# Attention with a SwiGLU feed-forward: keys as three chunks of 128 and a shared rest of 64, products in two banks

## The chip, the cores and the metric

The kernel runs on one core of a Trainium2 chip. The metric is the device time of one execution in microseconds (us), the median of several runs. The engines are TensorE (PE in the profile; PEld are its weight loads), VectorE (DVE), ScalarE (ACT), GpSimd (POOL) and SyncE (SP, which issues DMAs here).

## The reference

Multi-head attention over 8 batches of 12 heads, 448 positions of 64, then a feed-forward with a gate on the 3584 rows of 768. All tensors are float32; the kernel computes in float16 with float32 sums.

```python
q, k, v: (8, 12, 448, 64)
scores = np.matmul(q, k.transpose(0, 1, 3, 2)) / np.sqrt(64)
attn = softmax(scores)                                # over the keys
x = np.matmul(attn, v).transpose(0, 2, 1, 3).reshape(3584, 768)
g = x @ w_gate                                        # (768, 1536)
out = (g * sigmoid(g) * (x @ w_val)) @ w_out          # (1536, 768)
```

## The kernel before

Two heads make a pair: 48 pairs, six to a batch. Pair `pr` goes through these steps. Queries and keys are loaded as float16, position `4 p + c` at partition `p` of 112, chunk `c` of 4. They are turned so that the head dimension lies on partitions, head 0 on 0 to 63 and head 1 on 64 to 127 (on TensorE for the first pairs, by a DMA transpose from pair 11 on). `qk` makes the scores of one chunk of keys for both heads and takes their exponential:

```python
ps_s = ctx.enter_context(tc.tile_pool(name="ps_s", bufs=3, space=PSUM))   # tag "s": 3 tiles of two banks
ps_f = ctx.enter_context(tc.tile_pool(name="ps_f", bufs=2, space=PSUM))   # tag "f": 2 tiles of one bank

def qk(pr, c):                                  # c = 0..3, P = 112, S = 448, D = 64
    t = qkT[pr]
    s = ps_s.tile([128, 2, 512], FP32, tag="s")
    for hx in range(2):
        nc.tensor.matmul(                       # L217
            s[:, hx, 0:S],
            lhsT=t[ts(hx, 64), c * P : c * P + 128],
            rhs=t[ts(hx, 64), ds(S + (1 - hx) * D, S)],
            start=True,
            stop=True,
        )
    e = Es[pr % NE][:, ds(c * EB, 16)].rearrange("p (h b) x -> p h (b x)", h=2)
    nc.scalar.activation(e[:, :, 0:S], s[0:P, :, 0:S], AF.Exp, scale=sm_scale)      # L225
```

`pv_chunk` multiplies the exponentials with V. V has a column of ones behind its 64, so the sums of the softmax come with it as column 65. Both heads' 7 blocks of results (128 queries each; the last block holds the last 64 queries of both) lie in one bank, a tile of pool "f":

```python
def pv_chunk(pr, c):
    if c == 0:
        accs[pr] = ps_f.tile([128, 512], FP32, tag="f", name="acc")
    ...
    for j in range(3):
        for hx in range(2):
            nc.tensor.matmul(                   # L243
                a7[:, 2 * j + hx],
                lhsT=e[:, ds(c * EB + 9 * hx + 2 * j, 2)].rearrange("p b x -> p (b x)"),
                rhs=vo[:, hx, c, 0 : D + 1],
                start=c + j + hx == 0,
                stop=False,
            )
    for hx in range(2):
        nc.tensor.matmul(a7[:, 6], ...)         # L251
    if c < NC - 1:
        return
    ...
    nc.vector.reciprocal(r[:, 0:7], a7[:, :, D])          # L262
    nc.vector.tensor_tensor(xt[:, 0:n], a7[:, 0:n, 0:D], ..., ALU.mult)   # L264
```

The results are turned (`turn_x`, a DMA transpose from pair 12 on) into X, the input of the feed-forward. Its work is a list of steps. An FFN1 step takes one of 12 blocks of 128 hidden columns: six matmuls for the gate into `gp` (pool "s"), six for the value into `vp` (pool "f"), one activation on ScalarE and two operations on VectorE, of which the second, `hts`, reads `vp` out. An FFN2 step is twelve matmuls into `op` (pool "f"), which ScalarE copies to `osb`. The feed-forward of a batch's rows comes in blocks of 384 and of 512 rows.

The queues of all engines follow one list of visits. A visit has two or three chunks of scores, then the product of a pair whose exponentials are all there (none where no pair is ready), then some feed-forward steps of an earlier batch:

```python
for x, (chunks, todo) in enumerate(plan):
    for pr, c in chunks:
        qk(pr, c)
    ...
    for _, p0 in todo:
        pv(p0)
        ...
    if adds[max(y for y in adds if y <= x)] < 2:
        ...
        carry = run_budget(left() / (end - x) + carry)
    else:
        at, n = count["at"], count["visits"]
        no = share(count["o"], at, n)
        nf = 1
        ...
        for y in range(nf):
            if fvq:
                run_fv()
        for _ in range(no):
            run_o()
```

The last block of rows has nothing beside it and runs alone at the end.

Of the kernel before, what the change touches and what calls it, by code (L numbers as in the profile page):

```python
# [17 lines left out]
NB = 2  # L18
# [8 lines left out]
NX = 6  # L27
NV = 5
VS = 9
EB = 15  # L30


@with_exitstack
def kernel(
# [24 lines left out]
    MQ = S - D  # L59

# [22 lines left out]

    Es = [consts.tile([P, NC * EB + 1, D], FP16, name=f"E{i}") for i in range(NE)]
    Xts = [consts.tile([128, 7, D], FP16, name=f"xt{i}") for i in range(NX)]
    Xrs = [consts.tile([D, 128], FP16, name=f"xr{i}") for i in range(3)]
    Vts = [consts.tile([P, 2, NC, D + 2], FP16, name=f"vo{i}") for i in range(NV)]
    vraw = consts.tile([P, VS, 2, NC, D], FP16, name="vraw")
# [30 lines left out]

    def load_qk16(pr, n=2):  # L120
        h0 = 2 * (pr % 2) if pr >= 14 else 0
        if h0 == 0:
            q16 = raws.tile([P, 4, NC, D], FP16, tag="rq", bufs=RB, name="q16")
            k16 = raws.tile([P, 4, NC, D], FP16, tag="rk", bufs=RB, name="k16")
            pairbuf[:] = [q16, k16]
        q16, k16 = pairbuf
        for dst, src in ((q16, q), (k16, k)):
            flat = src.rearrange("b h s d -> (b h) s d")[2 * pr : 2 * pr + 2 * n]
            nc.gpsimd.dma_start(dst[:, ds(h0, 2 * n)], flat.rearrange("h (p c) d -> p h (c d)", c=NC))  # L129
        for i in range(n):  # L130
            h = h0 + 2 * i
            raw[pr + i] = (q16[:, h : h + 2], k16[:, h : h + 2])

    def load_v(pr, n=1):
        b, h = divmod(2 * pr, H)
        nc.gpsimd.dma_start(  # L136
            vraw[:, ds(pr % VS, n)].rearrange("p r h c d -> p (r h) (c d)"),
            v[b, h : h + 2 * n].rearrange("h (p c) d -> p h (c d)", c=NC),
        )

    def copy_v(pr):
        nc.vector.tensor_copy(Vts[pr % NV][:, :, :, 0:D], vraw[:, pr % VS])  # L142

# [12 lines left out]

    def prep(pr):
        rq, rk = raw[pr]
        if pr == 0 or pr >= NPE:
            qk16 = attp.tile([P, 2, NC, 2, D], FP16, tag="qk16", bufs=3)  # L160
# [7 lines left out]
        qkT[pr] = attp.tile([128, 2 * S + D], FP16, tag="qkT", name="qkT", bufs=5)  # L168
        if pr >= NPE:
            nc.sync.dma_start_transpose(  # L170
                qkT[pr][:, 0 : 2 * S].rearrange("p (c q) -> p c q", q=P),
                qk16[:].rearrange("p t c h d -> p (t c h d)"),
# [39 lines left out]

    def qk(pr, c):
        t = qkT[pr]
# [20 lines left out]
    def pv_chunk(pr, c):  # L235
# [3 lines left out]
        vo = Vts[pr % NV]  # L239
# [20 lines left out]
        r = attp.tile([128, 8], FP32, tag="R", bufs=2, name="R")  # L260
        xt = Xts[pr % NX]
        nc.vector.reciprocal(r[:, 0:7], a7[:, :, D])  # L262
        n = 7 if pr < XPE else 6
# [6 lines left out]
        if pr < XPE:  # L270
            return
        for hx in range(2):
            nc.vector.tensor_scalar(
                Xrs[pr % 3][:, ts(hx, D)], a7[ts(hx, D), 6, 0:D], r[ts(hx, D), 6:7], None, ALU.mult
            )

    def pv(pr):
        for c in range(NC):
            pv_chunk(pr, c)

    def turn_x(pr):
# [6 lines left out]
        if pr < XPE:  # L288
# [12 lines left out]
            dst[:, 0:MQ].rearrange("p (j q) -> p j q", j=3),  # L301
            xt[:, 0:6].rearrange("p j d -> p (j d)"),
        )
        nc.sync.dma_start_transpose(dst[:, MQ:S].rearrange("p (j q) -> p j q", j=1), Xrs[pr % 3][:])
# [48 lines left out]
    def ffn2_steps(kk, c0, n, hts, first, last_block):  # L353
# [6 lines left out]
        for ch, oh in steps:  # L360
# [7 lines left out]
            for m0, w in parts:  # L368
# [16 lines left out]
                while l < l0 + 128:  # L385
                    b, j = divmod(l, S)
                    c, p0 = divmod((j + D) % S, P)
                    m = min(P - p0, l0 + 128 - l, (MQ if j < MQ else S) - j)
# [16 lines left out]
    with tc.manual_schedule():  # L405
        load_qk32(0)
        nc.vector.memset(warm[:], 0.0)
        for e in Es:
# [41 lines left out]
        def add_block(i, visits):  # L450
# [5 lines left out]
            (oq if i == 0 else ffn2_wait).extend(own)  # L456
            count.update(visits=visits, fv=NFB, o=len(oq), at=0, more=NFB - visits)
# [53 lines left out]
        queue = []  # L511
        for p0 in range(FIRST, NPAIR):
            queue.append((NC * p0 + NC, p0))
        plan = []
        g = FIRST * NC
        last = NPAIR * NC
        while g < last or queue:
            n = 2 if g < WIDE * NC else 3
            todo = []
            while queue and queue[0][0] <= g and len(todo) < 2:  # L520
# [121 lines left out]
```

The softmax here doesn't subtract the row's maximum and nothing guards it: scores larger than these inputs give would overflow.

## Time and profile before

| | |
|---|---|
| median of 3 runs | 453.67 us (453.22 to 453.94) |
| span of the profiled execution | 451.7 us, 9871 instructions |
| score matmuls (L217) | 384, 50.6 us busy |
| product matmuls (L243, L251) | 1152 and 384, 53.0 and 42.9 us busy |
| FFN1 matmuls (L326), FFN2 matmuls (L371) | 1152 and 684, 249.3 and 116.1 us busy |
| exponentials (L225) | 192 of 919 ns |
| K, Q and V loads by GpSimd from DRAM | 44, 44 and 42 issues of some 0.66 us |

How to read it: busy time of an engine is the time in which at least one of its instructions is under way, and matmuls overlap, so a busy time divided by a count is not the time of one. A group's row gives line, engine, operation, output and input with their shapes, the count, busy us and the mean ns of one, and then how long the engine stood idle just before and what ended that. A row of waits gives who waited for what: us in total, times, longest. A row of a timeline gives start and length in us and how many instructions were merged into it. A row of windows gives the stretch, its length, then for PE, PEld, DVE, ACT and POOL the busy us and the count, and then the granted clock, the share of DMA and GB/s.

### The profile page before, as it was taken

To read this page: it belongs to the slowest core of one execution; us is meant where nothing else is said; L and a number is where in the kernel's file an instruction comes from. 1 tells how busy PE (TensorE), PEld (TensorE's weight loads), DVE (VectorE), ACT (ScalarE), POOL (GpSimd) and SP (SyncE) were. 2 spreads that over 40 slices of the span, in tenths; PEclk is the share of its full clock that TensorE was granted. 3 is DMA by queue.
4 is the path that set the end of the run, shared out by engine and by line. 5 is a ranking of instruction groups with operands and counts; after the bars stand their busy time and mean duration, and the time that the engine had idled before them with its cause. 6 is when DMAs were issued, how large, how long until landed. Compare 5 with 4: busy or idle time off the path is not lost.

```text
span 451.7 us, 9871 instructions
## 1 busy us (share of the span) xinstructions
PE 441.9 (98%) x4024; PEld 247.0 (55%) x4024; DVE 201.6 (45%) x447; ACT 238.8 (53%) x350; POOL 141.8 (31%) x228
## 2 busy tenths in 40 slices
PE   8999999999999999999999999999999999999995
PEld 3655565545455556454555656545455666544563
DVE  3666562456654434455443534353453544055300
ACT  6965666566746465554554546644555462222221
POOL 8755715927642225252313405330100000000000
PEclk9999999999999999999999999999999999999999
DMA  9999999999969379874749758772503112200033
GB/s 142 173 200 201 196 172 174 180 209 119 145 93 133 46 129 124 132 120 71 126 74 120 98 78 143 118 105 68 101 20 68 46 46 57 70 2 0 17 100 95
DMA packets 105101, 48.71 MB, mean 108 GB/s; under 512 B 59744, under 2 KB 101600, under 8 KB 105056
## 3 DMA queue, kind: packets, MB, share of 16 engines
q0 software_dynamic: 43392, 23.37, 41.2%
q1 hardware_dynamic: 61664, 24.71, 28.9%
q8 instruction: 31, 0.51, 0.5%
q14 instruction: 14, 0.11, 0.1%
HBM read 47.19 MB, written 11.01 MB: 129 GB/s over the span
## 4 chain that ended last, share of the span: by engine, by line
PE 93%; DVE 3%; ACT 2%; issue 1%; DVEq 0%; ACTq 0%
PE op L371 24%; PE gp L326 23%; PE vp L326 23%; PE s L217 9%; PE acc L243 9%; PE acc L251 2%; ACT E L225 2%; PE tp L208 1%; PE wp L109 1%; DVE t L345 1%; ACT sg L341 1%; DVE qkT L209 0%; DVE xt L264 0%; PE acc L291 0%; DVE hts L348 0%
## 5 line engine op out<-in xcount | busy, mean ns | idle before, releaser
L225 ACT ACTIVATE E<-s 112x896 f16<-112x896 f32 x192 | 162.1, 919 | 27.5 <-PE s L217 27.4
L326 PE MATMUL gp<-X,wg 128*128 128x384 f16 (+1 forms) x576 | 124.7, 352 | 0.0
L326 PE MATMUL vp<-X,wv 128*128 128x384 f16 (+1 forms) x576 | 124.6, 352 | 0.0
L371 PE MATMUL op<-wo,hts 128*128 128x384 f16 (+1 forms) x684 | 116.1, 323 | 0.0
L345 DVE SCALAR_TENSOR_TENSOR t<-sg,gp 128x384 f32<-128x384 f32 (+1 forms) x96 | 59.7, 621 | 121.8 <-ACT sg L341 121.8
L341 ACT ACTIVATE sg<-gp 128x384 f32<-128x384 f32 (+1 forms) x96 | 52.5, 547 | 84.8 <-PE gp L326 83.6
L371 PEld LDWEIGHTS <-hts 128*128 128x128 f16 x684 | 65.5, 98 | 45.9 <-issue 3.9
L326 PEld LDWEIGHTS <-wv 128*128 128x128 f16 x576 | 56.3, 98 | 52.6
L326 PEld LDWEIGHTS <-wg 128*128 128x128 f16 x576 | 53.1, 97 | 45.6 <-issue 1.1
L378 ACT ACTIVATE osb<-op 128x384 f32<-128x384 f32 (+1 forms) x57 | 27.8, 487 | 92.5 <-PE op L371 92.5
L167 POOL COPY qk<-q 112x512 f16<-112x512 f16 x37 | 22.9, 619 | 144.5 <-DMA qkT<-qk 143.1
L348 DVE SCALAR_TENSOR_TENSOR hts<-t,vp 128x384 f16<-128x384 f32 (+1 forms) x96 | 59.6, 621 | 10.0
L243 PEld LDWEIGHTS <-E 112*128 112x128 f16 x1152 | 46.7, 97 | 18.2 <-issue 17.5
L243 PE MATMUL acc<-vo,E 112*128 112x65 f16 x1152 | 53.0, 193 | 1.3 <-DVE vo L142 0.7
L217 PE MATMUL s<-qkT 64*128 64x448 f16 x384 | 50.6, 355 | 0.2
L251 PE MATMUL acc<-vo,E 112*128 112x65 f16 x384 | 42.9, 193 | 0.0
L262 DVE RECIPROCAL R<-acc 128x7 f32<-128x7 f32 x48 | 9.8, 205 | 70.6 <-PE acc L251 70.5
L129 POOL DMA_DIRECT2D k<-in_k_dram x44 | 29.0, 660 | 9.5 <-DMA wo<-in_moe_w_out_dram 7.8
L129 POOL DMA_DIRECT2D q<-in_q_dram x44 | 29.3, 666 | 5.2 <-PE s L217 2.5
L136 POOL DMA_DIRECT2D vraw<-in_v_dram x42 | 28.0, 666 | 8.4 <-DVE vo L142 7.2
L217 PEld LDWEIGHTS <-qkT 64*128 64x128 f16 x384 | 14.5, 94 | 25.8 <-issue 18.6
L264 DVE TENSOR_TENSOR xt<-acc,R 128x384 f16<-128x384 f32 (+1 forms) x48 | 27.6, 574 | 1.7
(41 smaller groups left out, 148.2 us busy)
## 6 DMA issues: line engine op xcount, KB each, us to landing
q<-in_q_dram POOLq DMA_DIRECT2D x41, 112.0 KB, 4.0
k<-in_k_dram POOLq DMA_DIRECT2D x41, 112.0 KB, 4.6
vraw<-in_v_dram POOLq DMA_DIRECT2D x39, 112.0 KB, 4.6
wg<-in_moe_w_gate_dram POOLq DMA_DIRECT2D x8, 288.0 KB, 10.1
wv<-in_moe_w_val_dram POOLq DMA_DIRECT2D x8, 288.0 KB, 10.2
wo<-in_moe_w_out_dram POOLq DMA_DIRECT2D x2, 1152.0 KB, 22.0
out_dram<-osb SPq DMA_DIRECT2D x8, 288.0 KB, 3.0
out_dram<-osb SPq DMA_DIRECT2D x8, 240.0 KB, 3.1
```

The costliest lines, as they stand in the source:

```text
L129: nc.gpsimd.dma_start(dst[:, ds(h0, 2 * n)], flat.rearrange("h (p c) d -> p h (c d)", c=NC))
L136: nc.gpsimd.dma_start(vraw[:, ds(pr % VS, n)].rearrange("p r h c d -> p (r h) (c d)"), v[b, h : h + 2 * n].rearrange("h (p c) d -> p h (c ...
L217: nc.tensor.matmul(s[:, hx, 0:S], lhsT=t[ts(hx, 64), c * P : c * P + 128], rhs=t[ts(hx, 64), ds(S + (1 - hx) * D, S)], start=True, stop=True,)
L225: nc.scalar.activation(e[:, :, 0:S], s[0:P, :, 0:S], AF.Exp, scale=sm_scale)
L243: nc.tensor.matmul(a7[:, 2 * j + hx], lhsT=e[:, ds(c * EB + 9 * hx + 2 * j, 2)].rearrange("p b x -> p (b x)"), rhs=vo[:, hx, c, 0 : D + 1] ...
L251: nc.tensor.matmul(a7[:, 6], lhsT=e[:, ds(c * EB + 6 + hx, 2)].rearrange("p b x -> p (b x)"), rhs=vo[:, hx, c, 0 : D + 1], start=False, st ...
L326: nc.tensor.matmul(dst[:, 0:n], lhsT=wslice(kind, fb, cb), rhs=X[kk][:, cb, ds(c0, n)], start=(cb == 0), stop=(cb == NCB - 1),)
L341: nc.scalar.activation(sg[:, 0:n], gp[:, 0:n], AF.Tanh, scale=0.5)
L345: nc.vector.scalar_tensor_tensor(t1[:, 0:n], sg[:, 0:n], 1.0, gp[:, 0:n], ALU.add, ALU.mult)
L348: nc.vector.scalar_tensor_tensor(hts[:, fb, 0:n], t1[:, 0:n], 0.5 * HS, vp[:, 0:n], ALU.mult, ALU.mult)
L371: nc.tensor.matmul(op[:, 0:w], lhsT=hts[:, fb, ts(ch, 128)], rhs=wo[oh][:, fb, ds(m0 - oh * OH, w)], start=(fb == 0), stop=(fb == NFB - 1),)
L378: nc.scalar.activation(osb[:, ds(m0, w)], op[:, 0:w], AF.Copy, scale=1.0 / HS)
```

## The change

From pair 12 on (batches 2 to 7) keys and values are cut otherwise. The 448 keys of a head are 64 groups of seven. They lie on 128 partitions: on the lower 64 the first four of each group, on the upper 64 the last four, so that the fourth is there twice. Of this three chunks of 128 keys and a rest of 64 are taken; of the two heads of a pair one has its rest on the lower half, the other on the upper. The rests of two pairs, four heads, fill one tile of scores and take one exponential. So two pairs have seven tiles of scores and seven exponentials instead of eight. The product of a pair goes into two banks, one per head, which are both tiles of pool "f" (the last two pairs take a tile of pool "s"). The products of the rest, which have 64 rows, come first and directly behind the scores of the visit, the two heads by turns.

With the larger chunks the list of visits is shorter, and from block 2 on the feed-forward steps are spread over the visits by their time; a visit ahead of a product gets an FFN2 step, which comes last in it, where there is one. K and V are loaded in two DMAs of 64 partitions each. The turning of keys and queries is two DMA transposes as before, cut otherwise. Output rows of batches 2 to 7 are in their natural order.

The diff, cut to its core:

```diff
+    def load_keys(eng, dst, src, h0, n):
+        for s in range(2):
+            rows = bass.AP(
+                src.tensor, (h0 * S + s * KR) * D, [[(2 * NC - 1) * D, 64], [S * D, n], [1, NC * D]]
+            )
+            eng.dma_start(dst[ts(s, 64)], rows)
+
+    def low(pr, hx):
+        return hx == pr % 2
...
+    def qk_quad(pr, c):
+        s = ps_s.tile([128, 2, 512], FP32, tag="s")
+        if c < KR:                                                   # KR = 3
+            t = qkT[pr]
+            for hx in range(2):
+                nc.tensor.matmul(
+                    s[:, hx, 0:S],
+                    lhsT=t[ts(hx, 64), ts(c + low(pr, hx), 128)],
+                    rhs=t[ts(hx, 64), ds(NC * 128, S)],
+                    start=True,
+                    stop=True,
+                )
+            e = Eq[pr % NE][:, c]
+        else:
+            for hx in range(2):
+                for p in (pr, pr + 1):
+                    lo = low(p, hx)
+                    t = qkT[p]
+                    nc.tensor.matmul(
+                        s[ts(1 - lo, 64), hx, 0:S],
+                        lhsT=t[ts(hx, 64), ds(0 if lo else KR * 128 + 64, 64)],
+                        rhs=t[ts(hx, 64), ds(NC * 128, S)],
+                        start=True,
+                        stop=True,
+                    )
+            e = Eq[pr % NE][:, RU]
+        nc.scalar.activation(
+            e[:, 0 : 2 * S].rearrange("p (h q) -> p h q", h=2), s[:, :, 0:S], AF.Exp, scale=sm_scale
+        )
...
+    def pv_mm(pr, hx, c, j):
+        lo = low(pr, hx)
+        first = not accs[pr][1][hx]
+        accs[pr][1][hx] += 1
+        if c < KR:
+            rows, e, col = slice(0, 128), Eq[pr % NE][:, c], c + lo
+        else:
+            rows, col = (slice(0, 64), 0) if lo else (slice(64, 128), KR)
+            e = Eq[(pr - pr % 2) % NE][:, RU]
+        nc.tensor.matmul(
+            accs[pr][0][hx][:, ts(j, D + 1)],
+            lhsT=e[rows, ds(hx * S + j * 128, 128)],
+            rhs=Vts[pr % NV][rows, hx, col, 0 : D + 1],
+            start=first,
+            stop=accs[pr][1][hx] == (KR + 1) ** 2,
+        )
...
+    def pv_open(pr):
+        if pr not in accs:
+            if wide(pr):                                             # the last two pairs
+                acc = ps_s.tile([128, 2, 512], FP32, tag="s", name="acc")
+                accs[pr] = ([acc[:, 0], acc[:, 1]], [0, 0], acc)
+            else:
+                accs[pr] = ([ps_f.tile([128, 512], FP32, tag="f", name="acc"), ps_f.tile([128, 512], FP32, tag="f", name="acc")], [0, 0])
+
+    def pv_piece(pr, c, heads=(0, 1)):
+        pv_open(pr)
+        for j in range(KR + 1):
+            for hx in heads:
+                pv_mm(pr, hx, c, j)
...
+    def pv_quad(pr):
+        for hx in range(2):
+            for c in range(KR):
+                pv_piece(pr, c, (hx,))
+        pv_close(pr)             # per head: reciprocal, then multiplication
...
+        def spread(i, x, visits):
+            ...
+            no = [int(x + y + 1 < len(plan) and bool(plan[x + y + 1][1])) for y in range(visits)]
+            ...
...
+            quads = [u for u in chunks if u[0] >= QUAD and u[1] == RU]
+            for pr, c in quads + [u for u in chunks if u not in quads]:
                 qk(pr, c)
+            for _, p0 in todo:
+                if p0 >= QUAD:                                       # QUAD = 12
+                    pv_piece(p0, RU)
...
-                at, n = count["at"], count["visits"]
-                no = share(count["o"], at, n)
-                nf = 1
-                ...
+                nf, no = steps.pop(0) if steps else (0, 0)
```

## The prediction

> **What bounds the kernel now.** I read the page first: busy time and chain.
>
> ```profile
> PE 441.9 (98%) x4024; PEld 247.0 (55%) x4024; DVE 201.6 (45%) x447; ACT 238.8 (53%) x350; POOL 141.8 (31%) x228
> ...
> PE 93%; DVE 3%; ACT 2%; issue 1%; DVEq 0%; ACTq 0%
> PE op L371 24%; PE gp L326 23%; PE vp L326 23%; PE s L217 9%; PE acc L243 9%; PE acc L251 2%; ACT E L225 2%; PE tp L208 1%; PE wp L109 1%; DVE t L345 1%; ACT sg L341 1%; DVE qkT L209 0%; DVE xt L264 0%; PE acc L291 0%; DVE hts L348 0%
> ...
> L225 ACT ACTIVATE E<-s 112x896 f16<-112x896 f32 x192 | 162.1, 919 | 27.5 <-PE s L217 27.4
> ```
>
> TensorE is busy 98% of the span and carries 93% of the chain that ended last. Everything else has room: the exponentials on ScalarE (L225), which the change makes fewer, are 162 us on an engine that is idle half the time. Next, what TensorE itself waits for, and the busy time of the stretch in which batch 6 is attended beside the feed-forward of earlier rows:
>
> ```profile
> PE wp L109 <- DVE warm L407: 1.2, 1, 1.2
> PE acc L291 <- DVE xt L264: 1.0, 1, 1.0
> PE acc L243 <- DVE vo L142: 0.7, 1, 0.7
> PE acc L243 <- DVE t L345: 0.4, 1, 0.4
> ```
>
> ```profile
> 286.90:341.70 54.80, 54.80 (x459) 27.91 (x456) 25.15 (x54) 29.70 (x43) 8.42 (x14) 1.00 0.41 76
> ```
>
> The named waits of TensorE are about 4 us in all and early; in the stretch TensorE (first pair of numbers after the length) is busy 54.80 of 54.80 us at the full clock (1.00), with DMA at 41%. So only TensorE time counts: the change is worth what it takes out of TensorE's instruction stream, less the waits it puts there. The last view is the timeline of one visit (three chunks of scores, one pair's product with V, then feed-forward):
>
> ```profile
> 324.68 1.46 PE L326 MATMUL gp<-X,wg 128*128 128x512 f16 x6
> ...
> 325.98 1.46 PE L326 MATMUL vp<-X,wv 128*128 128x512 f16 x6
> ...
> 327.37 0.74 PE L217 MATMUL s<-qkT 64*128 64x448 f16 x6
> 327.60 0.69 DVE L348 SCALAR_TENSOR_TENSOR hts<-t,vp 128x512 f16<-128x512 f32 x1
> ...
> 328.04 0.35 PE L243 MATMUL acc<-vo,E 112*128 112x65 f16 x6
> ...
> 329.02 1.46 PE L326 MATMUL gp<-X,wg 128*128 128x512 f16 x6
> ```
>
> Reading starts against starts: gp to vp is 1.30 us for six, 216 ns per 512 columns. vp to s is 1.39, so 0.09 to 0.10 more. The six score matmuls take 0.67 us: they run two heads at a time (rows 0 to 63 and 64 to 127), three rounds of 448 columns at 216 x 448/512 = 189 ns are 0.57, and again 0.10 is over. The 32 product matmuls (65 columns each) go from 328.04 to 329.02: 30.6 ns each. So each change between half-array and full-array matmuls costs about 0.10 us, and a visit with scores has two.
>
> **What the skill says.** (1) The Trainium skill, "TensorEngine Tiling (Array Packing)", Key Properties: changing the tiling mode drains the engine. The 0.10 us above agrees. (2) The same page, Gotcha 1: PSUM Pressure: different row tiles must write different banks. That is why the products go to two banks; the scores of before already do so. (3) "TensorE: Matmul & The Clock Gate", Back-to-back issue gap: N/2.4 + 2.5 ns, and a floor of some 25 ns per matmul. For 512 and 65 columns that is 216 and 29.6 ns; the trace has 216 and 30.6. The floor would forbid any gain from packing 65-column matmuls if it held across tiles. (4) The same page, Measured speedup vs the span model: matmuls in different row and column tiles run together, some 4 ns apart. For column halves the trace agrees:
>
> ```profile
> 17.98 0.39 PE L208 MATMUL tp<-ident,k 112*64 112x112 f16 x8
> ...
> 18.20 0.41 PE L208 MATMUL tp<-ident,q 112*64 112x112 f16 x10
> ```
>
> Eight transposes of 112 columns, alternating between the column halves, start within 0.22 us: 27 ns each, where 112 columns alone take 47. No run yet shows four quadrants at once.
>
> **The change part by part** (36 pairs, 12 to 47; the first 12 keep their code).
>
> Scores. Before, two pairs have 8 rounds of 189 ns. After, 6 chunks of 128 keys and one rest, whose four 64 x 64 matmuls occupy the four quadrants. If they run together, 7 rounds: 18 x 0.189 = 3.4 us saved. But quadrants are another tiling mode than row halves. The rest is put first in its visit, so full to quadrants replaces full to halves, and quadrants to halves is new: 18 x (0.095 + 3 x 0.004) = 1.9 us lost.
>
> Products. The count stays 32 per pair. 24 have 128 rows instead of 112 at the same 65 columns (no change); 8 have 64 rows, and two heads alternate between upper and lower rows and two banks. If they pair, 8 x 29.5 becomes 4 x 30 ns: 0.116 us per pair, 36 x 0.116 = 4.2 us saved. They stand directly after the scores, in the same row halves, so they add no mode change.
>
> Visits. At three units of scores per visit, 144 chunks are 48 visits and 126 are 42 (the instruction order of the two programs has these counts). Six fewer pairs of mode changes: 6 x 0.19 = 1.1 us saved. A product visit without scores at the end has two mode changes that it did not have: 0.2 us lost.
>
> Two banks. Pool "f" has two banks. Before, a pair's product took one, free for a while; now it takes both, and the second is the one that the step just before the scores used. Where that step is an FFN1 step, hts must have been read out: in the timeline it ends at 327.60 + 0.69 = 328.29, 0.92 us after the scores begin. The rest products now want the bank 0.57 us after the scores begin (0.67 in a visit with a rest of scores). With about 0.05 for the semaphore TensorE waits 0.4 (0.3) us. The new schedule puts an FFN2 step last ahead of a product to avoid just this, but during batch 2 none is available: six products follow vp there, 4 x 0.4 + 2 x 0.3 = 2.2 us lost. Behind an FFN2 step:
>
> ```profile
> 337.89 2.11 PE L371 MATMUL op<-wo,hts 128*128 128x384 f16 x12
> ...
> 339.94 0.74 PE L217 MATMUL s<-qkT 64*128 64x448 f16 x6
> 340.05 0.49 ACT L378 ACTIVATE osb<-op 128x384 f32<-128x384 f32 x1 [2.65 <-PE op L371]
> ```
>
> The bank is free at 340.54, 0.60 after the scores begin, against 0.57: with the semaphore 0.08 us in a visit without a rest, nothing with one. About 18 such visits: 1.4 us lost.
>
> Beside the path: 18 x 0.92 = 16.5 us fewer exponentials, DVE's close in two halves (about the 1.3 us of before per pair), 14% more K and V bytes, K and V loads as two DMAs each (two more issues of 0.66 us per pair on a POOL that is 31% busy), the same number of DMA transposes. The new sharing of FFN steps over the visits moves TensorE work without adding or removing any.
>
> Sum: -3.4 + 1.9 - 4.2 - 1.1 + 0.2 + 2.2 + 1.4 = -3.0 us. 453.7 - 3.0 = 450.7; I put 450.5, as the output of the last block is cut at fewer places.
>
> **Rivals.** (a) Packing fails: the rest products step at 30 ns each in spite of two banks, or the quadrants run two by two. For it: the floor in (3), and that no trace shows quadrants. Against: the score pairs and the column halves overlap. Without the product gain 454.7, without the score gain 453.9, without both 458. (b) The banks cost nothing: DVE and ScalarE finish a little earlier than I reckon, or the quadrant switch is free. Then -8.7 + 0.2 = 445.2. For it: the schedule was plainly reworked so that products follow FFN2 steps. Against: hts ends 0.92 us into the visit whatever is done, and batch 2 has no FFN2 steps. (c) Loads become the bound: more DMA issues on POOL, 64-partition halves, transposes asked for in another order. The DMA row has 9 tenths up to about 120 us, which is where pair 12 begins, so a late load could stop TensorE for some us there. Against: POOL runs several pairs ahead of TensorE, and keys of pair 12 and 13 are asked for at pair 4. It would give 452 to 456. (d) ScalarE becomes what sets a visit: the first gp behind a product needs the score tile whose exponential ends about 1.4 to 1.5 us after the scores begin. The shorter scores and products now reach it after 1.5 us, before after 1.65. It would eat the product gain in many visits, and give about 453.
>
> **Range and chances.** All gains together are 8.7 us, 1.9% of the time, so faster by 2% needs every gain whole and no wait: 0.04. Slower by 2% (462.7) needs a wait of half a microsecond in nearly every visit, such as a wrong guess about pool order or loads: 0.05. The rest is within 2%. Predicted 450.5, range 447 to 455.
>
> **What would show it.** Right: in the visits of batch 2 a gap of 0.3 to 0.4 us of TensorE between scores and products, released by DVE hts; hardly any in later batches; the four rest score matmuls starting within 0.02 us; eight rest products in 0.12 us; 0.1 us between quadrants and halves; ScalarE's exponentials down to about 146 us. Wrong: rest products in 0.24 us; the four rest matmuls spread over 0.2 us or more; waits of TensorE for a DMA transpose or for a V copy; a stretch of batches 3 to 6 in which TensorE has idle time.

## The result and the profile after

The changed kernel takes 452.09 us (median of 6 runs, 450.62 to 452.56), the kernel before in 6 runs 453.5 (453.2 to 453.94). The ratio is 0.9966, with a 95% interval of 0.9951 to 0.9982: a gain of a third of a per cent, of the 0.7% that was predicted. The profiled executions have spans of 451.7 before and 450.3 after.

The page of the kernel after, the rows that answer to those shown of before (busy time, chain by engine, exponentials):

```profile
PE 438.5 (97%) x4024; PEld 247.0 (55%) x4024; DVE 199.9 (44%) x447; ACT 224.8 (50%) x332; POOL 180.4 (40%) x299
...
PE 82%; DMA 9%; DVE 4%; ACT 2%; issue 1%; POOL 1%; SPq 0%; DVEq 0%; POOLq 0%
...
L283 ACT ACTIVATE E<-s 128x896 f16<-128x896 f32 x126 | 106.5, 922 | 14.4 <-PE s L262 9.2
```

TensorE is busy for 3.4 us less than before (441.9 to 438.5), but the span is only 1.4 shorter: TensorE stands idle for longer. The chain says where to look. It went over TensorE for 93% of the span and now does for 82%; 9% of it is DMA. GpSimd has 299 instructions instead of 228, 71 more, which are the additional load issues.

The waits of TensorE, after (us in total, times, longest):

```profile
PE op L510 <- DVE xt L398: 1.4, 1, 1.4
PE acc L356 <- DVE hts L487: 1.4, 7, 0.2
...
PE s L262 <- DMA qkT<-qk: 0.5, 1, 0.5
```

These three rows are new. The middle one is the second bank behind FFN1, which the prediction had. The first and the third occur once each, both near 80 us, where batch 2 begins. The timeline of that place, after (start, length, what; idle time and its releaser in brackets):

```profile
79.53 0.55 PE L262 MATMUL s<-qkT 64*128 64x448 f16 x4
...
80.58 0.37 PE L262 MATMUL s<-qkT 64*128 64x448 f16 x2 [0.49 <-DMA qkT<-qk]
...
80.77 1.14 PE L356 MATMUL acc<-vo,E 64*128 64x65 f16 x32
...
81.81 0.91 DVE L169 COPY vo<-vraw 128x512 f16<-128x512 f16 x1 [1.62 <-DMA vraw<-in_v_dram]
...
82.85 0.42 DVE L398 TENSOR_TENSOR xt<-acc,R 128x256 f16<-128x256 f32 x1
...
83.33 0.50 PE L510 MATMUL op<-wo,hts 128*128 128x384 f16 x2 [1.43 <-DVE xt L398]
```

First the scores wait 0.49 us for turned keys, those of pair 14. Then the product of pair 12 is done by 81.9, but VectorE, which must close it, has the copy of pair 13's V ahead of the close in its queue, and that copy waits 1.62 us for its load. So `xt` comes late, the FFN2 step, which needs the bank that `xt` is read from, waits 1.43 us, and the row of waits names VectorE for what is mostly a late load.

The two are late for different reasons. The issue of pair 13's V by GpSimd, before and then after:

```profile
72.77 0.66 POOL L136 DMA_DIRECT2D vraw<-in_v_dram  x1 [7.15 <-DVE vo L142]
```

```profile
76.07 1.22 POOL L132 DMA_DIRECT2D vraw<-in_v_dram  x2
```

In neither trace are more than eight loads of GpSimd under way at once. The weight `w_out` is loaded in two halves. Behind them six loads go out, and the next two stand until a half has landed (63.86 and 71.65 us after). Before, pair 12's V was among the six (54.80) and pair 13's V was the second of the two. After, four of the six are halves of keys, both halves of pair 12's V are what stands (64.39 and 71.93), and pair 13's V is asked for 3.3 us later than before. So this load is late because more issues stand ahead of it. The keys of pair 14 are not late: their turning is issued at 73.78 and 75.06 after, at 74.62 and 75.92 before. But their scores could start at 80.09 now, and in the kernel before they start at 84.75. Both are readings of the traces; no run changes one of the two alone.

The stretch with blocks 1 to 6 of the feed-forward, after it, in both kernels: before first, then after (length; PE, PEld, DVE, ACT, POOL busy; clock, DMA, GB/s):

```profile
86.40:393.80 307.40, 307.17 (x2692) 169.13 (x2689) 140.59 (x318) 165.97 (x245) 87.75 (x144) 1.00 0.64 100
```

```profile
89.00:394.00 305.00, 303.32 (x2688) 168.70 (x2685) 137.15 (x313) 152.05 (x227) 123.79 (x209) 1.00 0.73 104
```

This is where the change was to gain, and it does: 2.4 us. TensorE's busy time fell by 3.85, and 1.7 us of idle time stand against 0.2 before. From the start of block 1 to that of block 7 takes 305.03 to 305.04 us in every run below that leaves this stretch as it is (2, 7, 8, 9 and 10), so differences of a tenth of a us can be read there. In the stretch of one batch, the answer to the row shown of before:

```profile
288.30:342.60 54.30, 54.09 (x463) 27.94 (x460) 24.47 (x55) 27.29 (x40) 9.93 (x17) 1.00 0.42 73
```

0.2 us of idle time in a batch instead of none: small waits, and the full clock throughout.

Cut at the starts of feed-forward blocks (first gate matmul), the two profiled executions differ like this; each number is a difference of two start times of the traces:

| stretch | before | after | difference |
|---|---|---|---|
| start to block 1 | 86.40 | 89.00 | +2.60 |
| block 1 to block 7 | 307.43 | 305.04 | -2.39 |
| block 7 to the last matmul | 52.48 | 52.48 | 0 |
| last matmul to the end | 5.42 | 3.76 | -1.66 |

The last matmul starts no earlier than before (446.31 before, 446.51 after). What the scores and products gained was lost at 80 us, and the gain of the whole is made behind the last matmul. The first row of the table is not one fixed number: with the loads of the changed kernel block 1 begins at 89.00 in this profile and at 88.81, 89.72 and 90.30 in those of experiments 2, 5 and 3, but at 86.40 in both profiles with the old loads (before and experiment 1). The end, before:

```profile
445.18 3.69 SPq L390 DMA_DIRECT2D out_dram<-osb  x6
...
446.59 0.33 ACT L378 ACTIVATE osb<-op 128x192 f32<-128x192 f32 x1 [0.61 <-PE op L371]
```

and after:

```profile
443.74 3.73 SPq L530 DMA_DIRECT2D out_dram<-osb  x4
...
446.79 0.33 ACT L517 ACTIVATE osb<-op 128x192 f32<-128x192 f32 x1 [0.56 <-PE op L510]
...
447.15 0.38 ACTq L530 DMA_DIRECT2D out_dram<-osb  x1
```

Before, SyncE issues six stores in a row up to 448.87; the last issue ends 1.9 us after the data are in `osb` (446.92). After, one of the last two is issued by ScalarE, and both queues are done by 447.53.

What I held of it then: the change gains about 2.4 us in the steady part as reckoned, loses about as much at 80 us to loads that come late, and gains at the end by the other cut of the stores. The rivals: the gain of the steady part is of other make (products don't pack, waits are larger or smaller), or the end is not what its queues make it.

### The profile page after: what moved, and what is told of

It is laid out like the page before. It is cut to its first block, busy times and chain, and to the rows that moved or that the text cites. A ratio compares the mean times of both kernels' runs of the same rounds, so it can differ in the third digit from the quotient of the medians.

```text
span 450.3 us, 9959 instructions
## 1 busy us (share of the span) xinstructions
PE 438.5 (97%) x4024; PEld 247.0 (55%) x4024; DVE 199.9 (44%) x447; ACT 224.8 (50%) x332; POOL 180.4 (40%) x299
## 4 chain that ended last, share of the span: by engine, by line
PE 82%; DMA 9%; DVE 4%; ACT 2%; issue 1%; POOL 1%; SPq 0%; DVEq 0%; POOLq 0%
PE op L510 23%; PE gp L465 23%; PE vp L465 19%; PE acc L356 8%; DMA k<-in_k_dram 5%; PE s L262 4%; DMA q<-in_q_dram 2%; DVE t L484 2%; DVE hts L487 2%; PE s L293 1%; ACT sg L480 1%; PE acc L319 1%; DMA vraw<-in_v_dram 1%; PE s L275 1%; PE tp L252 1%
## 5 line engine op out<-in xcount | busy, mean ns | idle before, releaser
L283 ACT ACTIVATE E<-s 128x896 f16<-128x896 f32 x126 | 106.5, 922 | 14.4 <-PE s L262 9.2
L188 POOL COPY qk<-k 128x512 f16<-128x512 f16 x36 | 22.9, 637 | 98.6 <-DMA qkT<-qk 96.5
L132 POOL DMA_DIRECT2D vraw<-in_v_dram x72 | 44.1, 637 | 14.9 <-DMA k<-in_k_dram 6.9
L356 PE MATMUL acc<-vo,E 128*128 128x65 f16 (+1 forms) x1152 | 43.0, 193 | 1.7 <-DVE hts L487 1.4
L301 ACT ACTIVATE E<-s 112x896 f16<-112x896 f32 x48 | 40.7, 917 | 7.8 <-PE s L293 7.5
L356 PEld LDWEIGHTS <-E 128*128 128x128 f16 (+1 forms) x1152 | 37.2, 96 | 12.8 <-issue 7.1
L132 POOL DMA_DIRECT2D k<-in_k_dram x70 | 42.5, 623 | 2.1 <-DMA wv<-in_moe_w_val_dram 0.7
L397 DVE RECIPROCAL R<-acc 128x4 f32<-128x4 f32 x68 | 12.1, 177 | 61.3 <-PE acc L356 61.2
L398 DVE TENSOR_TENSOR xt<-acc,R 128x256 f16<-128x256 f32 x68 | 28.9, 425 | 2.3
L262 PE MATMUL s<-qkT 64*128 64x448 f16 x216 | 28.1, 353 | 0.5 <-DMA qkT<-qk 0.5
```

The costliest lines, as they stand in the source:

```text
L132: eng.dma_start(dst[ts(s, 64)], rows)
L188: nc.gpsimd.tensor_copy(dst.rearrange("p c h d -> p h c d"), src)
L262: nc.tensor.matmul(s[:, hx, 0:S], lhsT=t[ts(hx, 64), ts(c + low(pr, hx), 128)], rhs=t[ts(hx, 64), ds(NC * 128, S)], start=True, stop=True,)
L283: nc.scalar.activation(e[:, 0 : 2 * S].rearrange("p (h q) -> p h q", h=2), s[:, :, 0:S], AF.Exp, scale=sm_scale)
L356: nc.tensor.matmul(accs[pr][0][hx][:, ts(j, D + 1)], lhsT=e[rows, ds(hx * S + j * 128, 128)], rhs=Vts[pr % NV][rows, hx, col, 0 : D + 1], ...
```

## The experiments

**1. The end alone.** The kernel before, with the last stores shared out between the two queues:

```diff
-                    eng = nc.scalar if last and m < 64 else nc.sync
+                    eng = nc.scalar if last and l > l0 else nc.sync
```

> The kernel before, with one edit: of the two stores of each part of the last 128 rows, the second is issued by ScalarE instead of SyncE. Theory A (the change's 1.4 us come from the last stores, which happen to be cut 16 + 112 on two queues instead of 64 + 64 on one; the TensorE stream did not get shorter): 452.1 to 452.6 us, ratio about 0.997, last TensorE matmul unmoved. Theory B (the gain is in TensorE's stream): 453.5 us, ratio 1.000.

452.34 us against 453.54, ratio 0.9977 (0.9970 to 0.9983). The last matmul starts at 446.30 as before, and the end comes 4.46 us after it instead of 5.42. The end of this run:

```profile
445.17 2.41 SPq L390 DMA_DIRECT2D out_dram<-osb  x3
...
447.12 0.50 ACTq L390 DMA_DIRECT2D out_dram<-osb  x1
```

The queue of issues is over at 447.62 instead of 448.87. One line gives the old kernel 1.2 us, most of what the whole change gives. Then the reverse.

**2. The changed kernel with all stores on one queue.**

```diff
-                    eng = nc.scalar if last and m < 64 else nc.sync
+                    eng = nc.sync
```

> The changed kernel, with the stores of 16 rows of the last block issued by SyncE like those of 112, so that the end is on one queue as in the kernel before (though still cut 16 + 112). Theory A (the gain of the change is in the last stores): 0.4 to 1 us more than the changed kernel, 452.5 to 453.1, with the last TensorE matmul unmoved. Theory B: 452.1.

453.05 us (452.33 to 455.88), ratio 0.9997 (0.9982 to 1.0012), so no difference from the kernel before is left. But these times spread over 3.5 us, and the profiled execution shows that one queue gives back only a part: the last matmul starts at 446.32, and the end comes 4.27 after it, 0.51 more than in the changed kernel. Its six issues:

```profile
445.19 2.65 SPq L530 DMA_DIRECT2D out_dram<-osb  x6
```

Six in a row take 2.65 us where they took 3.69 before: issues of 16 and 112 rows are 0.31 to 0.43 us each, those of 64 rows 0.47 to 0.60. From the last matmul to the end, the four kernels have:

| | one queue | two queues |
|---|---|---|
| cut 64 + 64 | 5.42 (before) | 4.46 (experiment 1) |
| cut 16 + 112 | 4.27 (experiment 2) | 3.76 (after) |

So the gain of 1.66 behind the last matmul has two parts, the cut (0.70 to 1.15) and the second queue (0.51 to 0.96). Both come of the order of the output rows: it cuts the last 128 rows into 16 and 112, and the line `m < 64`, which both kernels have, then sends the 16 to ScalarE. Nothing in the arithmetic of the scores and products has part in it.

**3. The rest products by head.** The changed kernel issues the rest products with the two heads by turns. Here it issues all of one head, then all of the other:

```diff
-                    pv_piece(p0, RU)
+                    pv_piece(p0, RU, (0,))
+                    pv_piece(p0, RU, (1,))
```

> The changed kernel, with the rest products of one head after those of the other instead of by turns, so that no two neighbours lie in different row halves. If packing is worth what the prediction said (0.116 us per pair), 36 pairs cost 4.2 us more, less about 0.1 us at each of some 10 long waits for the second bank, which four products can now precede: 455 to 456 us against 452.1. If packing is worth nothing (a floor per matmul): 452 or a little less. The eight rest products should start over 0.23 us instead of 0.12.

452.32 us, ratio 0.9984 (0.9967 to 1.0000); from block 1 to block 7 it takes 305.21 us against 305.04. The expected loss did not come, and the trace says why. Where the second bank was free in time, the eight rest products still start 8 to 21 ns apart, within 0.112 us in all: the upper and the lower row half work side by side although the program puts four matmuls of one before four of the other (the second head's first starts before the first head's fourth). Where the second bank was late, four step at 29 ns, then comes a step of 0.30 us, then four step at 29 ns, and from the last score matmul to the last product it is the same 1.50 us both ways, as half of the work is done in the wait. So this was no test of packing, as the edit does not undo it. It does show that the overlap comes of the row halves, not of the order. No run takes the packing away; what it is worth is read from the traces of before and after.

Packing itself is seen directly. A visit with a rest of scores, after:

```profile
119.36 0.38 PE L275 MATMUL s<-qkT 64*64 64x448 f16 x4
119.68 0.55 PE L262 MATMUL s<-qkT 64*128 64x448 f16 x4
...
120.07 1.38 PE L356 MATMUL acc<-vo,E 64*128 64x65 f16 x32
```

The four rest score matmuls start 3 to 4 ns apart and leave room for the next after 0.31 us: the four quadrants run together. In visits with a free bank, the eight rest products start within 0.096 us, and from the last score matmul to the step behind the product it is 1.14 us instead of 1.26 before.

**4. The rest products between the heads.** The rest no longer stands behind the scores but between the whole chunks of head 0 and of head 1. Then the second bank is wanted 0.35 us later, but each pair has two more changes between half and full array:

```diff
-        for hx in range(2):
-            for c in range(KR):
-                pv_piece(pr, c, (hx,))
+        for c in range(KR):
+            pv_piece(pr, c, (0,))
+        pv_piece(pr, RU)
+        for c in range(KR):
+            pv_piece(pr, c, (1,))
...
-            for _, p0 in todo:
-                if p0 >= QUAD:
-                    pv_piece(p0, RU)
```

> The changed kernel, with the rest products between the whole chunks of head 0 and those of head 1, instead of directly behind the scores. Head 0's bank is free when the scores end, and by the time the rest wants the second bank 0.46 us more have gone. Theory (waits for the second bank are 4.5 us in all, a change between half and full array 0.094 us): waits under 0.1 us everywhere, less 4.2 us; two more mode changes per pair, 36 x 0.19 = 6.8 us more; 2.6 us slower, 454.7 us. Rival (the 0.39 us gaps are mode changes or weight loads and not the bank): the gaps stay, 458 us or more.

455.04 us, ratio 1.0032 (1.0019 to 1.0045). From block 1 to block 7 it takes 307.74 us, 2.70 more than after. No product of the new form waits for `hts` any more, and the additional changes cost more than that. Only the difference of the two is measured; it is what the reckoning of both gave (2.6). Putting the rest behind the scores is the better trade.

**5. The old sharing of feed-forward steps.** The changed kernel with the code of before that spreads FFN1 and FFN2 steps over the visits in place of `steps.pop`:

> The changed kernel, with the feed-forward steps shared out as before (one FFN1 step per visit, the rest to visits with an FFN2 step) instead of by their time. Theory (all that the new sharing does for TensorE is to put FFN2 steps ahead of products): 13 products follow an FFN1 step instead of 11, 2 x 0.3 = 0.6 us more, 452.7 us. Rival (visits of unequal length make ScalarE late): TensorE waits for exponentials, over 454 us.

452.49 us, ratio 0.9986 (0.9969 to 1.0004), so by time alone nothing is decided. The stretch from block 1 to block 7 decides: 305.69 us, 0.65 more. The new order, which puts an FFN2 step last ahead of a product, spares about that much waiting.

**6. FFN2 steps for batch 2.** If steps of FFN2 are kept back until batch 2, its products need not follow FFN1:

```diff
-            (oq if i == 0 else ffn2_wait).extend(own)
-            if i >= 2 and x is not None:
+            ffn2_wait.extend(own)
+            if i >= 1 and x is not None:
...
-            if adds[max(y for y in adds if y <= x)] < 2:
+            if adds[max(y for y in adds if y <= x)] < 1:
```

> The changed kernel, with the six FFN2 steps of block 0 kept for the visits of batch 2, and the spreading used from block 1 on. Theory A (the waits for the second bank behind FFN1 steps and the FFN2 step directly behind the product of pair 12 are real losses): four of the six waits of 0.3 to 0.4 us in batch 2 shrink to under 0.1, and the 1.4 us wait of op for xt goes: 1.2 + 1.4 = 2.6 us less, about 449.5 us. Rival (the start is bound by loads): batch 2 begins 12 us earlier, keys or values come late, TensorE waits for a DMA for some us, and the time is 452 to 458.

460.03 us, ratio 1.0137 (1.0121 to 1.0152). With FFN2 work moved behind the start of block 1, TensorE runs ahead of its loads. The waits of TensorE in this run:

```profile
PE xtp L427 <- DVE xt L340: 2.9, 1, 2.9
PE s L275 <- DMA qkT<-qk: 2.5, 2, 2.0
...
PE s L262 <- DMA qkT<-qk: 1.1, 1, 1.1
```

Six FFN2 steps of 1.95 us, 11.7 us in all, were moved into block 1. It takes 54.3 us instead of 44.1, so 1.5 less than the moved work: the gaps behind FFN1 are gone but for one of 0.395, as theory A had it. The loss lies ahead: from block 0 to block 1 it takes 57.08 us instead of 59.16, although 11.7 us of work are missing there. TensorE waits for loads, and for 10.2 us of this stretch the granted clock is at half. The work that was taken away had given the loads their time. The rival had this one.

**7. V of pairs 12 and 13 earlier.** The wait at 80 us is released by a V load. Here both are asked for ahead of the first half of `w_out`:

```diff
-            6: [("V", 3), ("o", 0)],
+            6: [("V", 3), ("v1", 12), ("v1", 13), ("o", 0)],
...
-                if 12 <= pr + 3 < NPAIR:
+                if 14 <= pr + 3 < NPAIR:
```

> The changed kernel, with V of pairs 12 and 13 asked for ahead of the first load of w_out instead of three pairs ahead. Theory A (the 1.4 us wait of op for xt is a V load that landed late: VectorE's copy of V stood ahead of the close of pair 12 in its queue; and the 0.5 us wait of scores for a transposed key has the same backlog on GpSimd behind it): both go, 450.2 to 450.7 us, ratio to the changed kernel 0.996. Rival (op waits for the close of the product in any case, as both banks are taken): the op wait stays at 0.8 us or more, 451.5.

453.78 us, ratio 1.0008 (1.0000 to 1.0016): slower than after by 1.7. Its waits of TensorE:

```profile
PE s L293 <- DMA qkT<-qk: 2.7, 1, 2.7
...
PE s L275 <- DMA qkT<-qk: 0.9, 1, 0.9
...
PE op L510 <- DVE xt L398: 0.4, 1, 0.4
```

The wait of 1.4 for the close fell to 0.4, and keys, which now stand behind V, cost 3.6. Block 1 begins at 91.63 instead of 89.00.

**8. The copy of V behind the products.** The load stays, but VectorE no longer stands in front of it:

```diff
-            for p0 in vcopies.get(x, []):
-                copy_v(p0)
             ...                                   # scores, products and closes of the visit
+            for p0 in vcopies.get(x, []):
+                copy_v(p0)
```

> The changed kernel, with VectorE's copy of the next V put behind the close of the product of the same visit, instead of ahead of it; nothing else is moved. Theory A (op waits 1.4 us for xt of pair 12 because a late V load holds the copy, and the copy holds the close): the op wait falls to about 0.4 us (a close takes 0.2 + 0.4 us and the last 12 products 0.36), the late V is needed only 5 us later, and the time is about 451.0 us. Rival (both banks are taken, so op waits for the close in any case): the op wait stays above 1 us, 452.1 us.

451.49 us, ratio 0.9955 (0.9942 to 0.9969). The place at 80 us in this run:

```profile
80.91 0.37 PE L262 MATMUL s<-qkT 64*128 64x448 f16 x2 [0.99 <-DMA qkT<-qk]
...
82.60 1.31 PE L510 MATMUL op<-wo,hts 128*128 128x384 f16 x7 [0.37 <-DVE xt L398]
...
83.08 0.46 DVE L169 COPY vo<-vraw 128x512 f16<-128x512 f16 x1
```

The copy now comes after the close, and the wait of 1.43 is 0.37. So 1.06 of the 1.43 was the late V, and 0.37 stays, as both banks are taken until the close. The wait for keys, 0.49 after, is 0.99 here. Block 1 begins at 88.45, so 2.0 of the 2.6 us are still lost. The five times (451.24 to 452.14) lie within those of the changed kernel (450.62 to 452.56): the shorter wait is shown, a shorter time is not.

**9. Keys earlier.** With the copy behind, keys of pair 14 are copied and turned one pair sooner:

```diff
-                lead = [pr + 3] if pr + 3 < QUAD else [pr + 3, pr + 4] if pr + 3 == QUAD else [pr + 4]
+                lead = [pr + 3] if pr + 3 < QUAD else [pr + 3, pr + 4, pr + 5] if pr + 3 == QUAD else [pr + 4] if pr > 10 else []
```

> The changed kernel, with the copy of V behind the close (as in the run before) and pair 14's keys turned one pair earlier, ahead of the V loads that hold GpSimd's queue until w_out has landed. Theory A: the wait of scores for a DMA of some 0.5 to 1 us at 80 us goes, the op wait stays at 0.4: block 1 begins at about 87.3, 450.3 us. Rival (memory traffic is the limit until 120 us, so that what is asked for earlier makes something else late): another wait for a DMA takes its place, 451 to 454 us.

454.01 us, ratio 1.0002 (0.9989 to 1.0015); block 1 at 91.33. The timeline of GpSimd in this run:

```profile
73.06 0.62 POOL L188 COPY qk<-k 128x512 f16<-128x512 f16 x1 [16.61 <-DMA k<-in_k_dram]
```

GpSimd issues the loads and also makes copies. Asked for sooner, the copy of pair 14's keys stands 16.61 us for a load that is itself behind `w_out`, and everything GpSimd has to issue behind it is late. A wait moved from keys to V (2.0 us of TensorE for pair 12), and behind it the clock falls, as the last section shows.

**10. The second half of `w_out` later,** with the copy behind:

```diff
-            7: [("o", 1)],
+            9: [("o", 1)],
```

> The changed kernel, with the copy of V behind the close and the second half of w_out asked for two pairs later, behind the keys of pairs 14 and 15 and V of pair 12. Theory A (the late keys and values at 80 us stand behind the 2.4 MB of w_out in the memory queue): no wait of scores for a DMA at 80 us, only the 0.4 us of op for the close: block 1 begins at about 87.2, 450.2 us. Rival (what is put back comes late itself): the FFN2 steps of the second half, at about 74 us, wait for w_out, and block 1 begins at 89 or later.

452.37 us, ratio 0.9976 (0.9966 to 0.9985), not better than 8. Its waits of TensorE:

```profile
PE op L510 <- DMA wo<-in_moe_w_out_dram: 0.9, 1, 0.9
...
PE op L510 <- DVE xt L398: 0.4, 1, 0.4
```

Keys at 80 us are in time now, and an FFN2 step waits for `w_out` instead; block 1 begins at 88.29, hardly sooner than in 8. Three ways of shifting loads (7, 9, 10), and each turned one wait into another.

**11. More issues alone.** In the kernel before, K and V from pair 12 on loaded as 64 and 48 partitions: the same bytes, twice the issues of these loads, nothing else changed. K is shown; V is cut in the same manner, and Q goes through the same lines uncut:

```diff
-            nc.gpsimd.dma_start(dst[:, ds(h0, 2 * n)], flat.rearrange("h (p c) d -> p h (c d)", c=NC))
+            src = flat.rearrange("h (p c) d -> p h (c d)", c=NC)
+            cuts = ((0, 64), (64, P)) if pr >= 12 and dst is k16 else ((0, P),)
+            for a, z in cuts:
+                nc.gpsimd.dma_start(dst[a:z, ds(h0, 2 * n)], src[a:z])
```

> The kernel before, with K and V of pairs 12 to 47 loaded in two DMAs of 64 and 48 partitions each, so with the 70 more issues of GpSimd that the change has, and nothing else of it. Theory A (the late data at 80 us is because the new order of scores wants pair 14 a visit earlier, not because of the number of issues): block 1 begins within 0.3 us of 86.4, 453.5 us. Rival (the issues make the loads late): block 1 begins 1 to 2.5 us later, 454.5 to 456 us.

457.44 us, ratio 1.0087 (1.0067 to 1.0108). From block 1 to block 7 it takes 307.43 as before, and block 1 begins at 90.47, 4.07 later. GpSimd and then TensorE in this run:

```profile
64.12 0.60 POOL L140 DMA_DIRECT2D vraw<-in_v_dram  x1 [8.57 <-DMA wo<-in_moe_w_out_dram]
...
70.04 0.56 POOL L140 DMA_DIRECT2D vraw<-in_v_dram  x1 [5.32 <-DMA wo<-in_moe_w_out_dram]
```

```profile
PE s L221 <- DMA qkT<-qk: 2.2, 1, 2.2
```

Issues of GpSimd wait for loads of `w_out` to land, 8.57 and 5.32 us, and the copies of pair 13's keys come at 70.6 instead of 55.45. So issues alone, without a byte more, can cost this much at this place. Of the 4.07 us, 2.2 are the wait; some 1.6 (an estimate: 3.24 us of work at half the clock) come of the clock behind it, as the last section shows. I had thought too little of it beforehand. It is not the same loss as in the changed kernel, where pair 13's keys are copied in time, at 54.51 us, and what is late is V of pair 13. That issues alone make the loss there is not shown: it also asks for pair 14 one visit sooner, and has 14% more bytes.

**12. The new cut from batch 3 on.** If the loss comes of starting the new loads while `w_out` is on its way, it should go away when batch 2 keeps the old form. The changed kernel, with the two heads' last blocks of pairs 12 to 17 written separately so that the turning of later pairs fits:

```diff
-QUAD = 12
+QUAD = 18
...
-    n = 7
+    n = 7 if pr < XPE else 6
...
+    if pr < XPE:
+        return
+    for hx in range(2):
+        nc.vector.tensor_scalar(
+            xt[0:D, 6 + hx], a7[ts(hx, D), 6, 0:D], r[ts(hx, D), 6:7], None, ALU.mult
+        )
```

> The changed kernel, with the new keys and products from pair 18 on (batch 3) instead of 12; batch 2 is attended as in the kernel before. Theory A (the change gains in every stretch except where batch 2 begins, as transposed keys and values of its first pairs land too late there): block 1 of the feed-forward begins at 86.4 us as in the kernel before (89.0 in the changed one) and takes 43.5, blocks 2 to 6 take the changed kernel's 260.9, the end stays short: 448.8 us, ratio to before 0.990. Rival (the gain and loss are spread, or the first pairs of the new form lose wherever they begin): block 2 begins late in its turn and the time is 451 to 452.

449.51 us (449.41 to 449.87) against 453.5, ratio 0.9916 (0.9902 to 0.9929): faster than both kernels, by less than 1%. Its waits of TensorE have no row with a DMA in them and none for `op`; of the new rows only this is left:

```profile
PE acc L362 <- DVE hts L493: 0.9, 5, 0.2
```

Block 1 begins at 86.42, where it began before (86.40). Block 1 itself takes 44.0 us and blocks 2 to 6 take 260.9, together 304.9: nothing of the steady gain is lost, although six of the 36 pairs stay in the old form. In batch 2, which has no FFN2 steps to put ahead of its products, the new form had gained nothing: block 1 takes 44.1 us with it in the changed kernel, 44.0 without it here, and 43.5 in the kernel before.

## Why the prediction was right, and where it was not

The time (450.5 predicted, range 447 to 455, measured 452.09) and "within 2%" held, and the terms for TensorE's stream held with small errors. Two other terms were sized far too small, +2.6 at the start and -1.66 at the end, and they cancel in part. That is luck: without the end the time would have been about 453.7 (452.09 + 1.66), no gain at all. Rival (c) gave 452 to 456, which has the measured time in it as well, and its sign, waits for a DMA transpose and for a V copy, is what the profile shows. Step by step, for the stretch between blocks 1 and 7 first:

- Scores, -3.4: right. The rest matmuls of four heads start 3 to 4 ns apart; quadrants do run together, which no trace had shown. Rival (a) falls.
- Quadrants to halves, +1.9: 306 ns from the last rest matmul to the next, 117 more than the 189 of a round. With the 10 ns of spread this is 0.127 x 18 = 2.3.
- Products, -4.2: right, 8 in 0.12 us where the bank is free (0.096 for the eight starts, and 0.12 to the next, of which 0.09 are the change of mode). The floor of 25 ns per matmul that the Trainium skill gives ("TensorE: Matmul & The Clock Gate", Back-to-back issue gap) does not hold across row halves.
- Visits, -1.1: 42 instead of 48, and a change of mode measures 0.093 to 0.096 us. It was not tried by itself; nor was the +0.2 for a visit without scores.
- Second bank behind FFN1, +2.2: right for the six visits that I counted. Their gaps are 0.40, 0.39, 0.39, 0.27, 0.40 and 0.27, in sum 2.1. The view is the timeline of a visit of batch 2, after:

```profile
100.08 1.46 PE L465 MATMUL vp<-X,wv 128*128 128x512 f16 x6
...
101.47 0.74 PE L262 MATMUL s<-qkT 64*128 64x448 f16 x6
...
101.70 0.69 DVE L487 SCALAR_TENSOR_TENSOR hts<-t,vp 128x512 f16<-128x512 f32 x1
...
102.05 0.19 PE L356 MATMUL acc<-vo,E 64*128 64x65 f16 x1
...
102.45 1.11 PE L356 MATMUL acc<-vo,E 64*128 64x65 f16 x31 [0.20 <-DVE hts L487]
...
103.39 1.46 PE L465 MATMUL gp<-X,wg 128*128 128x512 f16 x6
```

  The first product starts, the second head's waits until `hts` is out at 102.39: 0.40 from 102.05 to 102.45. The bracket and the row of waits put only half of it down to VectorE. In a gap behind an unfinished matmul, starts against starts are the better reading.
- Missed: four later products wait 0.34 to 0.40 too, 1.46 in all. The visit before them has scores but no product, and in such a visit the FFN2 step is run first, so it ends in FFN1 as well. I took the rule "FFN2 last" as holding for all visits of later batches. In return two waits of the kernel before in batch 2, 0.37 together, are gone.
- Second bank behind FFN2, +1.4: 14 waits of 0.064 us, 0.9.
- Rivals (b) and (d): banks do cost, and no wait for ScalarE appears. The exponentials come down from 162.1 to 147.2 us (106.5 of the new form and 40.7 of the old twelve pairs; about 146 was expected).

In sum -3.4 + 2.3 - 4.2 - 1.1 + 2.1 + 0.9 + 1.46 - 0.37 = -2.3, and the stretch measures -2.39. That the sum fits so well has some luck in it, as visits of pairs 12 and 13 lie ahead of the stretch. Experiment 4 traded one of these terms against another, and 5 changed one; both gave what the terms say.

What failed:

- "Loads become the bound", rival (c), was in the prediction with a size of nothing. It is +2.6 us at 80 us. Its argument against ("POOL runs several pairs ahead, and keys of pair 12 and 13 are asked for at pair 4") looked at the two pairs that were asked for early; it was pair 14's keys that were wanted sooner and pair 13's V that came late. Nor does pair 12 begin at about 120 us, where the full DMA row ends: its scores start at 72 us before, in the middle of it. That GpSimd is busy for 31% of the span did not say that it has room at 57 to 72 us, when its issues stand behind `w_out` (7.75 and 7.15 us already in the kernel before). Experiment 12, where the loss goes away whole, shows that it belongs to the new form in batch 2; 11 shows that issues alone can cost as much, through another load. In 7, 9 and 10 a new order of the loads only decided who waits. In the profiled execution the 2.6 us hold 0.49 for keys that are wanted a visit sooner, 1.06 for V that is asked for later, as more issues stand ahead of it, and 0.37 because both banks are taken until the close. Some 0.7 stays open; 0.3 of it is there when pair 12's scores begin (72.03 instead of 71.72).
- "-0.2, as the output of the last block is cut at fewer places": the place was right and the size was not, it is -1.66. I counted cuts and looked neither at what an issue of 64 rows takes nor at who issues the last store. Experiments 1 and 2 show the two parts.

Without these two terms the change would be worth the 2.4 us of the stretch. With the loss avoided and the end kept it is worth 4.0, as experiment 12 has it; 1.66 of that is the end, and one line gives the old kernel 0.96 of it (experiment 1).

## What to carry to other kernels

When a change is reckoned in the steady part, look separately at the first use of the new form and at the last store: each is used once, and here they were 2.6 and 1.7 us, against 2.4 from the pairs. Where loads are tight for a stretch, do not begin a form with more loads there; begin it a stage later, since shifting single loads in the queue only changes which engine waits. And where a copy that waits for a load stands ahead of urgent work in its engine's queue, try the order on that engine before the load (here one moved line took the wait from 1.43 to 0.37 us).

## What was not expected of the hardware

- Matmuls of two row halves run side by side even when the program puts all of one half before all of the other (eight starts within 0.112 us, experiment 3). There a matmul of the second half starts ahead of one that stands before it in the program.
- From quadrants to row halves costs 0.117 us, from halves to the full array and back 0.093 to 0.096.
- After the wait of 2.2 us in experiment 11 TensorE is slow for a while: 32 products step at 55 ns instead of 29. The granted clock (the number after POOL's) is at half there:

```profile
77.50:80.50 3.00, 3.00 (x37) 2.23 (x38) 0.56 (x2) 0.92 (x1) 3.00 (x7) 0.50 1.21 181
```

  In experiment 9 it is at half from 84.0 to 87.3, behind the wait of 2.0. It need not be so: in experiment 7 a wait of 2.7 us ends at 69.2, and the clock stays full.

```profile
69.00:72.00 3.00, 2.79 (x45) 1.92 (x46) 0.83 (x2) 2.39 (x3) 0.00 (x0) 1.00 1.28 190
```

  So a wait of 2 us can cost more than its length, and the length alone does not tell whether it will.
- Issuing the last stores took SyncE 0.47 to 0.60 us for 64 rows and 0.32 for 112 (0.42 behind an issue of 16, experiment 2); ScalarE took 0.50 to 0.55 for 64 and 0.38 to 0.39 for 16.
